# A decode step with sliding-window attention and an MLP on one Trainium2 core: fewer loads for the last weights, more loads for a bias, and a new order of the closing products

## The chip, the core and the metric

The kernel runs on one core of a Trainium2 chip (trn2). The metric is the device time of one execution in microseconds (us). Engines: PE multiplies matrices, PEld is its weight load, DVE, ACT and POOL work element by element, SP (SyncE) issues DMAs. A DMA is cut into packets that 16 DMA engines move.

## What is computed

Eight tokens (batch 8, one position, width 448) go through two branches, and a gate mixes them.

```python
g = sigmoid((x * gate_w).sum(-1, keepdims=True))
q = (x @ wq)                                  # 16 heads of 256
k, v = k_cache[:, :, -1024:], v_cache[:, :, -1024:]   # 8 KV heads, each for 2 query heads
a = (softmax(q k^T / 16) v) @ wo              # wo is 4096 x 448
b = gelu(layernorm(x) @ w1 + b1) @ w2 + b2    # hidden width 1792
out = g * a + (1 - g) * b
```

Weights and caches are bfloat16. The two windows of the caches are 67 MB of the 77.85 MB that the profile shows moved.

## The kernel before

**Loads.** All large loads go through SP's queue, in the order of a list called `plan`. A load fills a slot; a slot is 32 KB on each of 128 partitions (4 MB in all), and four slots form a ring (`RING = 4`, lines 98 to 118). `pump()` issues loads until four slots are ahead of what has been consumed; `done()` counts a slot as consumed and calls `pump()`. The plan is: wq (three DMAs), the eight blocks of keys k0 to k7, from k4 on with the values between them (k4, v0, k5, v1, k6, v2, k7, v3), then v4 to v6, w1 in two DMAs, v7 together with w2, and last wo. `rows_loader` (lines 138 to 146) issues one DMA for each piece of a list; line 143 is the issue.

**wo** is cut by `wo_v` (line 153) into four blocks q = 0 to 3, and each block into eight groups j = 0 to 7: on each partition a group is one row of 448 numbers (896 bytes), 112 KB over 128 partitions. The list `cuts` (lines 172 to 179) makes eight DMAs of it: block 0, block 1, groups 0 to 3 and 4 to 7 of block 2, and of block 3 the groups 0 to 1, 2 to 5, 6, and 7.

**Biases.** `biases()` (lines 193 to 201) is called after the keys k1 have been turned, just behind the issue of v0. It loads b2 into eight partitions with two DMAs of four rows each (line 195) and b1 with four DMAs of one row each (line 201). They are first used by `norm()` (line 318), called after the values of batch 4.

**DMA semaphores.** Every DMA names a semaphore that tells of its landing. The framework gives out eight of them; in the trace they are 100, 102, 103, 104, 105, 108, 109 and 110. The stretch around the biases and the last loads, from the trace's records of instructions and semaphore updates (us from the start of the span; "landed" is the last update before the next use):

| DMA | issued | semaphore | landed |
|---|---|---|---|
| k3 | 15.47 | 100 | 51.71 |
| k4 | 31.38 | 102 | 61.38 |
| v0 | 42.88 | 103 | 71.06 |
| b2, two DMAs | 43.55, 44.12 | 104, 105 | 70.72, 70.91 |
| b1, first three | 44.43, 44.72, 45.02 | 108, 109, 110 | 70.31, 70.49, 70.67 |
| b1, fourth | 51.73 | 100 | 70.86 |
| k5 | 61.46 | 102 | 80.73 |
| v1 | 71.15 | 103 | 90.54 |
| wo blocks 0, 1 | 158.70, 159.08 | 109, 110 | 177.80, 179.94 |
| wo block 2, two halves | 159.56, 160.03 | 100, 102 | 181.01, 182.11 |
| wo block 3, groups 0-1, 2-5 | 161.64, 162.21 | 103, 104 | 182.71, 183.81 |
| wo block 3, group 6, group 7 | 171.97, 175.69 | 105, 108 | 184.09, 184.37 |
| out by ACT, out by SP | 185.13, 185.12 | 109, 110 | 186.37, 186.55 |

**The closing products** (lines 688 to 740). `chunks` is a list of 46 products that are all summed into the output: 14 with w2, then 32 with wo, block by block and group by group. The last `TAIL` of them are `narrow`, the others `wide`. A wide product is one matmul over 448 columns into `A1`; four in a row go to four groups of output partitions (`g = i % QD`). DVE then adds the bias into `accs` (line 719). A narrow product is two matmuls over 224 columns, into `A2[0]` or `A2[1]` as the list `part` says, and each of the four combinations has its own group of output partitions. `pick` times `accs`, in float32, brings the wide sum into the narrow one; it stands at place `EARLY` of the narrow list. When the products for `A2[1]` are done, DVE copies them to `early` (line 737), beside the rest of those for `A2[0]`; `res` (line 738) adds the two, and SP and ACT each store a half. `FILL` says after how many wide products how many extra matmuls into an unused tile (`run_on`, tile `warm`) are run; they compute nothing that is used.

Of the kernel before, what the change touches and what calls it, by code (L numbers as in the profile page):

```python
# [17 lines left out]
def kernel(  # L18
# [18 lines left out]
    NB, Sq, D = A_x.shape  # L37
# [8 lines left out]
    QD = 4  # L46
# [11 lines left out]
    QN = 512  # L58
# [6 lines left out]
    J8 = Dh // BL  # L65
    NQW = Hq // QD
# [6 lines left out]
    CK = SLOT // Dh  # L73
    KQ = W // (KS * CK)
    HR = GROUP * UR
    TAIL = 12
    SHIFT = 96
    EARLY = 4
    TURNED = {5: 3, 6: 3, 7: 3}
    FAR = -3.0e38  # L80
    FILL = {0: 3, 14: 5, 22: 4, 30: 1, 34: 1}
    qscale = float(Dh) ** -0.5

    xf = A_x.rearrange("b s d -> (b s) d")
# [28 lines left out]
    def add(key, loader):  # L113
        index[key] = len(plan)
        plan.append(loader)

    def slot(*key):
        return slots[index[key]]
# [49 lines left out]
    for b in range(KQ, NB - 1):  # L168
        add(("v", b), pair_loader(A_v_cache, b))
    add(("w12",), rows_loader([w1_m, w1_t]))  # L170
    add(("v", NB - 1), last_values)
    cuts = [(q, 0, J8) for q in range(NQW - 2)] + [
        (NQW - 2, 0, 4),
        (NQW - 2, 4, 8),
        (NQW - 1, 0, 2),
        (NQW - 1, 2, 6),
        (NQW - 1, 6, 7),
        (NQW - 1, 7, 8),
    ]
# [7 lines left out]
    b2_b = consts.tile([NB, D], BF16)  # L187
# [3 lines left out]
    )  # L191

    def biases():
        for o in range(0, NB, QD):
            nc.sync.dma_start(
                b2_b[o : o + QD, :],
                B_b2.rearrange("(o d) -> o d", o=1).to_broadcast([QD, D]),
            )
        parts = B_b1.rearrange("(t d) -> t d", t=QD)
        for t in range(QD):  # L200
            nc.sync.dma_start(b1_r[BL * t : BL * t + 1, :], parts[t : t + 1, :])
# [26 lines left out]
    for u in range(NG):  # L228
        o = u * BL
# [429 lines left out]
    for m in range(NK):  # L659
        transpose_keys(m, steps(m - KQ) if m >= KQ else {})  # L660
        if m == 1:
            biases()
        if m < KQ:
            turn_blocks(m + 1)
        if m == 0:
            gate()
        scores(m)
        if m % KQ == KQ - 1:
            top(m // KQ)
        if m >= KQ:  # L670
            values(m - KQ)
# [23 lines left out]
    ] + [(oP[:, c % J8, c // J8, :], w[:, c * D : (c + 1) * D]) for c in range(NCH)]  # L695
    wide, narrow = chunks[:-TAIL], chunks[-TAIL:]

    def run_on(n, m=QN):
        for _ in range(n):
            nc.tensor.matmul(  # L700
                warm[:, 0:m],
                lhsT=ident[:],
                rhs=slot("v", NB - 1)[:, 0:m],
                start=True,
                stop=True,
            )

    run_on(FILL[0])
    for i, (lhsT, rhs) in enumerate(wide):
# [7 lines left out]
        )  # L717
        run_on(FILL.get(i + 1, 0))
    nc.vector.tensor_tensor(accs[:], A1[:], b2s[:], op=ALU.add)
    narrow.insert(EARLY, (pick[:], accs[:]))  # L720
    part = [1, 0, 1, 0, 0, 1, 1, 0, 0, 0, 0, 0, 0]
    early = consts.tile([2 * BL, DO], F32)
    res = consts.tile([2 * BL, DO], BF16)
    for i, (lhsT, rhs) in enumerate(narrow):
        k = part[i]
        for h in range(2):
            g = 2 * k + h
            nc.tensor.matmul(
                A2[k][BL * g : BL * g + NB, :],
                lhsT=lhsT,  # L730
                rhs=rhs[:, h * DO : (h + 1) * DO],
                start=(k not in part[:i]),
                stop=(k not in part[i + 1 :]),
            )
        if 1 not in part[i + 1 :] and k == 1:
            run_on(1, QN // 2)
            nc.vector.tensor_copy(early[:], A2[1][2 * BL : P, :])
    nc.vector.tensor_tensor(res[:], A2[0][0 : 2 * BL, :], early[:], op=ALU.add)
    for h, eng in enumerate((nc.sync, nc.scalar)):
# [31 lines left out]
```

## Time and profile before

| | |
|---|---|
| median of 3 runs | 189.46 us (189.45 to 189.76) |
| the profiled execution's own time | 189.29 us |
| its span in the profile | 187.4 us |
| bytes moved, mean rate | 77.85 MB, 415 GB/s |
| PE, DVE, POOL, ACT busy | 67%, 50%, 43%, 39% of the span |
| mean granted TensorE clock | 0.851 |
| last load landed, end of the span | 184.37 us, 187.39 us |

All profile times count from the start of the span. The execution is 1.9 us longer than its span and 0.17 us under the median. A name such as `slot<-in_A_wo_dram` reads as written<-read; L143 is a line of the kernel; SPq is SP's queue of instructions.

### The profile page before, as it was taken

Reading aid. Unit: us, or ns where it says so; the run is one execution under the profiler, and the core shown is the slowest. Engines: PE = TensorE matmul, PEld = TensorE weight load, DVE = VectorE, ACT = ScalarE, POOL = GpSimd, SP = SyncE. Lnnn points to the kernel's source line nnn. Section 1 sums busy time; section 2 is a strip of 40 time slices with the busy share of each in tenths; the row PEclk is TensorE's granted clock in tenths of the full one; section 3 lists DMA queues with packets and bytes.
Section 4 is the critical chain, followed back from the end, with each engine's and each line's share of the span. In section 5 each row is a group of like instructions: output and inputs, shape, how many; then the busy total and the mean of one; then the engine's idle time right before and its main releaser. Section 6 shows DMA issues by size and latency. Waiting matters only on the chain.

```text
span 187.4 us, 2775 instructions
## 1 busy us (share of the span) xinstructions
PE 125.4 (67%) x1102; PEld 73.0 (39%) x1103; DVE 94.0 (50%) x161; ACT 72.4 (39%) x87; POOL 80.8 (43%) x157
## 2 busy tenths in 40 slices
PE   0252498998988988489877985984670167543983
PEld 0010485675756746253752572563120022111321
DVE  6602247664654566770662281493044982347611
ACT  2003379692855929740680373184025010001000
POOL 8401591671927639103996899299900000000000
PEclk9999579999999999756997899999576576855798
DMA  6999999999998999999999999999999999999991
GB/s 223 444 455 448 448 434 413 388 442 448 444 448 381 418 439 435 430 416 455 451 416 402 434 458 441 392 441 427 430 430 423 434 430 428 432 430 418 421 406 65
DMA packets 5443, 77.85 MB, mean 415 GB/s; under 512 B 540, under 2 KB 1080, under 8 KB 1848
## 3 DMA queue, kind: packets, MB, share of 16 engines
q1 hardware_dynamic: 5384, 77.68, 97.2%
q8 instruction: 8, 0.13, 0.2%
q10 hardware_dynamic: 48, 0.02, 0.0%
q14 instruction: 3, 0.02, 0.0%
HBM read 77.69 MB, written 0.01 MB: 415 GB/s over the span
## 4 chain that ended last, share of the span: by engine, by line
DMA 46%; PE 25%; ACT 12%; DVE 7%; POOL 5%; issue 2%; SPq 1%; POOLq 0%; ACTq 0%; DVEq 0%
DMA slot<-in_A_k_cache_dram 22%; PE ktp L390 15%; DMA slot<-in_B_w_dram 12%; DMA slot<-in_A_wo_dram 12%; ACT kt L394 9%; PE S_ps L465 7%; POOL kt L369 5%; DVE kt L396 3%; PE PO L550 2%; DVE B L355 1%; ACT E L489 1%; ACT other L489 1%; SPq L143 1%; DVE EB L505 1%; DVE E L503 1%
## 5 line engine op out<-in xcount | busy, mean ns | idle before, releaser
L369 POOL COPY kt<-B 32x128 f32<-32x128 f32 (+1 forms) x128 | 72.4, 566 | 42.8 <-PE S_ps L465 24.9
L390 PE MATMUL ktp<-ident_f,slot 128*128 128x128 f32 x456 | 64.6, 292 | 14.0 <-DMA slot<-in_A_k_cache_dram 5.9
L394 ACT COPY kt<-ktp 128x1024 bf16<-128x1024 bf16 x57 | 56.3, 1015 | 45.8 <-PE ktp L390 45.7
L390 PEld LDWEIGHTS ktp<-ident_f,slot 128*128 128x128 f32 x456 | 52.4, 148 | 27.7 <-ACT kt L394 11.3
L396 DVE COPY kt<-ktp 128x1024 bf16<-128x1024 bf16 x57 | 39.0, 689 | 32.0 <-PE ktp L390 31.6
L465 PE MATMUL S_ps<-kt,qw 128*16 128x512 bf16 x256 | 21.1, 458 | 12.1 <-POOL kt L369 9.3
L550 PE MATMUL PO<-slot,ET 128*16 128x512 bf16 x256 | 22.2, 508 | 6.6 <-DMA slot<-in_A_v_cache_dram 3.0
L355 DVE STREAM_TRANSPOSE B<-slot 128x512 f32<-128x512 f32 (+1 forms) x8 | 8.8, 1105 | 14.2 <-DMA slot<-in_A_k_cache_dram 9.7
L465 PEld LDWEIGHTS <-qw 128*16 128x16 bf16 x256 | 6.6, 92 | 23.8 <-issue 13.3
L550 PEld LDWEIGHTS <-ET 128*16 128x16 bf16 x256 | 7.9, 112 | 19.3 <-issue 12.9
L525 PE MATMUL sm<-EZ,perm 128*128 128x128 bf16 x8 | 2.0, 248 | 13.4 <-DVE EZ L512 13.4
L407 PE MATMUL S_ps<-slot,xw 128*8 128x512 bf16 x24 | 2.9, 618 | 10.7 <-DVE xw L254 7.1
L478 DVE TENSOR_REDUCE nmx<-S_ps 128x1 f32<-128x2048 f32 x2 | 4.6, 2292 | 9.8 <-PE S_ps L465 9.8
L565 DVE STREAM_TRANSPOSE T<-PO 128x512 f32<-128x512 f32 x8 | 5.7, 707 | 7.6 <-PE PO L550 7.6
L627 ACT ACTIVATE zb<-za 128x448 f32<-128x448 f32 x1 | 0.6, 576 | 18.8 <-DVE za L626 18.8
L489 ACT ACTIVATE E<-S_ps,nmx 128x1024 f32<-128x1024 f32 x2 | 4.1, 2031 | 9.7 <-DVE nmx L478 9.7
L525 PEld LDWEIGHTS <-perm 128*128 128x128 bf16 x8 | 0.8, 100 | 16.6 <-DVE EZ L512 16.6
L445 POOL COPY qw<-qt 32x64 bf16<-32x64 bf16 x8 | 2.2, 277 | 11.3 <-DVE qt L432 11.0
L533 DVE TENSOR_TENSOR ET<-sm,mask 128x512 bf16<-128x512 f32 x8 | 5.5, 687 | 1.1 <-PE sm L525 1.0
L432 DVE STREAM_TRANSPOSE qt<-qs 128x512 bf16<-128x512 bf16 x2 | 1.3, 690 | 8.8 <-ACT qs L429 8.8
L407 PEld LDWEIGHTS <-xw 128*8 128x8 bf16 x24 | 0.7, 100 | 12.0 <-POOL b_r L237 7.1
L700 PE MATMUL warm<-slot,ident 128*128 128x512 bf16 (+1 forms) x14 | 4.3, 392 | 0.1
(91 smaller groups left out, 69.0 us busy)
## 6 DMA issues: line engine op xcount, KB each, us to landing
slot<-in_A_k_cache_dram SPq DMA_DIRECT2D x8, 4096.0 KB, 24.6
slot<-in_A_v_cache_dram SPq DMA_DIRECT2D x8, 4096.0 KB, 30.0
slot<-in_A_wq_dram SPq DMA_DIRECT2D x1, 2048.0 KB
slot<-in_A_wo_dram SPq DMA_DIRECT2D x2, 896.0 KB
slot<-in_B_w_dram SPq DMA_DIRECT2D x1, 1568.0 KB
slot<-in_B_w_dram SPq DMA_DIRECT2D x1, 1344.0 KB
slot<-in_A_wo_dram SPq DMA_DIRECT2D x3, 448.0 KB, 22.1
slot<-in_A_wq_dram SPq DMA_DIRECT2D x1, 1024.0 KB
```

The costliest lines, as they stand in the source:

```text
L355: nc.vector.transpose(B[:].rearrange("p c w x -> p (c w x)"), kn[:, 0 : n * P],)
L369: nc.gpsimd.tensor_copy(words[BL * w : BL * (w + 1), BL * g : BL * (g + 1), 0:n, 0], B[BL * g : BL * (g + 1), :, w].rearrange("p c x -> p ...
L390: nc.tensor.transpose(words[:, c, :, 0], kn[:, o : o + P], ident_f[:])
L394: nc.scalar.copy(dst, src)
L396: nc.vector.tensor_copy(dst, src)
L465: nc.tensor.matmul(S_ps[BL * t : BL * t + HR, k * QN : (k + 1) * QN], lhsT=qf[:, o : o + HR], rhs=KT[0][:, x : x + n, :, j], start=False, ...
L478: nc.vector.reduce_max(nmx[:], S_ps[:], axis=AXIS.X, negate=True)
L489: nc.scalar.activation((E[:, 0:W], other[:])[u].rearrange("p (c k s) -> p k s c", k=KQ, c=NCK), S_ps[:].rearrange("p (k u s c) -> p u k s ...
L533: nc.vector.tensor_tensor(ET[:].rearrange("p c u a r -> p (c u) a r"), sm[:] .rearrange("p k (o r) -> p k o r", o=1) .to_broadcast([P, NCK ...
L550: nc.tensor.matmul(PO[BL * t : BL * t + Hq], lhsT=ET[:, c].rearrange("p u a r -> p (u a r)"), rhs=vn[:, c], start=(c < QD), stop=(c >= NCK ...
L565: nc.vector.transpose(T[:, 0 : NG * n], PO[:].rearrange("p u (e j) -> p u j e", j=J8))
L700: nc.tensor.matmul(warm[:, 0:m], lhsT=ident[:], rhs=slot("v", NB - 1)[:, 0:m], start=True, stop=True,)
```

## The change

wo comes in six DMAs: blocks 0, 1 and 2 whole, and of block 3 the groups 0 to 5, 6, and 7. b2 comes in four DMAs of two rows in place of two of four rows. The narrow list now has the 16 products of blocks 2 and 3, with `pick` times `accs` ahead of them; the products of block 2 go to `A2[0]` and `A2[1]` by turns, group 0 of block 3 closes `A2[1]`, and groups 1 to 7 go to `A2[0]`. Four fillers stand after the last wide product (there was one after product 30 and one after product 34), and the short filler stands after block 2.

```diff
-    TAIL = 12
+    TAIL = 16
-    EARLY = 4
+    EARLY = 0
-    FILL = {0: 3, 14: 5, 22: 4, 30: 1, 34: 1}
+    FILL = {0: 3, 14: 5, 22: 4, 30: 4}
...
-    cuts = [(q, 0, J8) for q in range(NQW - 2)] + [
-        (NQW - 2, 0, 4),
-        (NQW - 2, 4, 8),
-        (NQW - 1, 0, 2),
-        (NQW - 1, 2, 6),
+    cuts = [(q, 0, J8) for q in range(NQW - 1)] + [
+        (NQW - 1, 0, 6),
         (NQW - 1, 6, 7),
         (NQW - 1, 7, 8),
     ]
...
     def biases():
-        for o in range(0, NB, QD):
+        for o in range(0, NB, 2):
             nc.sync.dma_start(
-                b2_b[o : o + QD, :],
-                B_b2.rearrange("(o d) -> o d", o=1).to_broadcast([QD, D]),
+                b2_b[o : o + 2, :],
+                B_b2.rearrange("(o d) -> o d", o=1).to_broadcast([2, D]),
             )
...
-    part = [1, 0, 1, 0, 0, 1, 1, 0, 0, 0, 0, 0, 0]
+    part = [1] + [0, 1] * 4 + [1] + [0] * 7
...
+        if i == J8:
+            run_on(1, QN // 2)
         if 1 not in part[i + 1 :] and k == 1:
-            run_on(1, QN // 2)
             nc.vector.tensor_copy(early[:], A2[1][2 * BL : P, :])
```

## The prediction

> **What bounds the kernel now.** I read the page first, then the chain of waits, then SP's own waits and its timeline, and last the trace's packets and semaphore updates for the moments at which loads land.
>
> ```profile
> span 187.4 us, 2775 instructions
> ...
> DMA  6999999999998999999999999999999999999991
> ...
> q1 hardware_dynamic: 5384, 77.68, 97.2%
> ```
>
> The DMA engines are busy from the second slice to the last but one, and SP's queue alone holds them for 97.2% of the span. No engine of the first list is over 67%. So the stream of loads is the bound, and a moment in which it stands still is not won back. The landings say the same: k5, v1 and the blocks after them land 9.66 to 9.81 us apart up to the last values (80.73, 90.54, 100.20, 109.89 ... 158.36).
>
> The chain in its window from 139 us ends so:
>
> ```profile
> 139.89 22.30 DMA slot<-in_B_w_dram
> 162.19 0.02 issue
> 162.21 21.60 DMA slot<-in_A_wo_dram
> 183.81 0.04 issue
> 183.85 0.84 PE S_ps L728 x12
> 184.69 0.02 issue
> 184.71 0.38 DVE res L738
> ```
>
> The end is the landing of wo plus about half a microsecond of products, an addition and the store. Two places can therefore move the time: the rate and the gaps of the stream, and the piece behind the last landing.
>
> How SP feeds the stream stands in its waits between 40 and 72 us (total, times, longest), and in its timeline there:
>
> ```profile
> SPq L126 <- DMA slot<-in_A_k_cache_dram: 9.4, 1, 9.4
> SPq L134 <- DMA slot<-in_A_v_cache_dram: 9.1, 1, 9.1
> SPq L201 <- DMA slot<-in_A_k_cache_dram: 6.4, 1, 6.4
> ```
>
> ```profile
> 42.88 0.62 SPq L134 DMA_DIRECT2D slot<-in_A_v_cache_dram  x1
> 43.55 0.83 SPq L195 DMA_DIRECT2D b_b<-in_B_b_dram  x2
> 44.43 7.53 SPq L201 DMA_DIRECT2D b_r<-in_B_b_dram  x4
> 61.46 0.55 SPq L126 DMA_DIRECT2D slot<-in_A_k_cache_dram  x1
> 71.15 0.62 SPq L134 DMA_DIRECT2D slot<-in_A_v_cache_dram  x1
> ```
>
> The four loads of b1 take 7.53 us to issue, because the fourth waits 6.4 us for a load of keys with which it shares no data. What it shares is the semaphore: its number 100 was k3's, which landed at 51.71, and the load starts at 51.73. Then k5 waits 9.4 us for k4 (semaphore 102, landed 61.38), and v1 waits 9.1 us for v0 (103, landed 71.06). The eight semaphores go round, and **a DMA waits until the DMA eight places ahead of it has landed**. SP issues in order, so what stands behind waits too. Now this costs nothing: when k5 is issued at 61.46, v0 still has 9.6 us to run.
>
> **The change part by part.**
>
> *wo in six DMAs.* Block 1 takes 179.94 − 177.80 = 2.14 us. The halves of block 2 take 1.07 and 1.10, so one load saves 0.03. Groups 0-1 and 2-5 of block 3 take 0.60 and 1.10; six groups at the rate of block 1 take 6/8 x 2.14 = 1.61, which saves 0.09. Together −0.12 us at the last landing. SP's two spared issues (0.33 us each) lie where it is idle (158 to 176 us).
>
> *The closing products.* Wide products now end with block 1's (180.57, end of L711's group), then `accs` (0.62) is ready at about 181.25. PE passes four fillers until 181.6 (four took 1.04), and `pick` times `accs` (0.54) ends near 182.15. Block 2 lands near 182.1: at most 0.1 us late for eight products that need four steps of 0.095 us (the spacing of the pairs of L728), in front of a landing that comes 1.6 us later. That interval covers the added fillers and the short one. Without it, three more fillers would cost 0.65. Behind the landing T of the six groups, group 0 runs beside group 1 in another group of output partitions (as the first four matmuls of L728 started within 0.01 us), so group 7 starts at T + 0.04 + 6 x 0.095 = T + 0.61. It lands at T + 0.56 and could start at T + 0.60. That is +0.01; if the two don't run beside each other, +0.1. `early` ends at T + 0.04 + 0.26 + 0.05 + 0.39 = T + 0.74, before `res` can start at T + 0.90 (184.71 − 183.81), so it stays hidden by 0.16.
>
> *b2 in four DMAs.* By themselves two more issues of 0.26 us, on an SP that then waits anyway. But they move all that follows two places on in the round. Behind v0 on 103 come b2 on 104, 105, 108, 109 and b1 on 110, 100, 102, 103. The second b1 waits for k3 (51.71), the third for k4 (61.38), **the fourth for v0 itself, 71.06**. Queued behind it on SP is k5, whose slot was free before 61.4, and nothing else is left for the DMA engines. The gap, step by step: the fourth b1 is issued 71.08 to 71.33 (0.25 each now); k5 starts at about 71.42. From issue to the first packet, the trace shows 0.8 (the store: 185.12 to 185.91) to 1.0 (the first load: 0.73 to 1.74), and the first packets of an idle engine took 0.15 to 0.35 us longer than later ones. So the engines work fully from 72.2 to 72.8; I take 72.5.
>
> Now twelve of the sixteen engines start on k5 at 69.05 to 69.86, the other four at 70.19 to 70.71. The gap is 2.6 to 3.4 us for the twelve and 1.8 to 2.3 for the four. Which of them sets the end? v0's landings show twelve engines 1.3 us or more ahead of the last one; at the last load (183 to 184 us) only five are still 1.0 ahead, and nine lie within 0.35 of the last. Between, single engines lose about 1.4 us each around five packets of the queue "q8 instruction" (87.5, 103.8, 120.8, 139.6, 168.9), and fall back to the latest. After the gap all start level, and the engines that lose 1.4 later come last. For those the shift is 72.5 − 69.35 = 3.15. If no such loss followed, it would be 72.5 − 70.71 = 1.8. I take 3.1, nearest to what the packets of this trace did.
>
> The Trainium skill, page "DMA: Bandwidth & Descriptors", section "Latency and other measured facts", gives 0.6 us to the first byte of a load issued from SP. By it the restart would be 0.2 to 0.4 us earlier and the sum about 0.3 lower; the 0.8 to 1.0 of the trace decides.
>
> *Sum:* −0.12 + 0.01 + 3.1 = +3.0 on the profiled execution's 189.29, so 192.3. That execution lies 0.17 under the median of 189.46; between the two bases I write **192.4**.
>
> **The rivals.**
>
> 1. *The gap costs less* (chance 0.15). SP stalls, but the engines' later losses don't repeat, or fall on engines with time to spare: 1.8 − 0.1 on 189.46 gives 191.1, with the earliest restart 190.8. For it speaks that the lateness never exceeds that of the latest engine in the trace of before; against it, that four or more engines did lose over 1.1 us after 71 us.
> 2. *The gap costs more* (0.04). PE's granted clock drops to 0.5 in part of the last slices (the PEclk row has 5s and 7s there); shifted against the products, half speed adds 6 x 0.095 = 0.6 behind the last landing: 193.0. The latest restart (72.8) with 3.4 gives 193.3, with both 193.6.
> 3. *The round is not what I read from it* (0.09). If the fourth b1 does not share v0's semaphore, SP is free before 61.46 and only −0.12 + 0.01 is left: 189.3, within what can be told. For it: only the trace, not the code, shows who assigns semaphores. Against: every DMA from k3 on follows the round.
> 4. *Faster* (0.04). It needs rival 3's free SP, and a price per load in the stream of more than 0.19 us, since two loads are spared and 0.38 is 0.2%. Where it would be: at the end, each load paying its time from issue to first packet, 0.8 to 1.0. Two fewer give −1.6 to −2.0, 187.5. Against it: the halves of block 2 land 1.10 us apart, for 1.07 at block 1's rate, so the border costs 0.03. The Trainium skill, same page, section "Anatomy of one DMA — SWDGE (gpsimd) path", has for loads from GpSimd a fit of 2.0 us for each DMA plus its bytes over 436 GB/s; by that rule two fewer would bring 4.0 us. The landings of the two halves speak against it here.
>
> **How the numbers follow.** The forecast has 0.68; its own range is 191.6 (restart 72.2 and a loss after it of 1.0) to 193.3. Slower by over 0.2% (0.38 us, about what a measurement of this kernel can tell from no change) is 0.68 + 0.15 + 0.04, and a stall by another place in the round adds 0.01: 0.88. Same 0.08, faster 0.04. The range 190.8 to 193.6 takes in the forecast and rivals 1 and 2, 0.87 in all; the no-stall cases lie outside.
>
> **What would show it.** In SP's timeline the loads of b1 stretch from 45 to 71 us, k5 is issued near 71.4, and SP's wait at L201 for v0 is new, about 9.4 us. In the DMA row one slice near 72 us falls from 9 to about 4 or 5. k5 lands near 83.5, not 80.7, and the last load near 187.4. Wrong from the root would be k5 issued before 62 us; wrong in size, a last landing under 186.5. The closing part is right if the last landing and the start of `res` stay 0.3 to 0.4 us apart, and blocks 2 and 3 up to group 5 land 2.14 and 1.6 us after what precedes them.

## The result and the profile after

The changed kernel takes 195.41 us (median of 5 runs, 195.04 to 195.43), the kernel before 189.45 beside it: a ratio of 1.0305, 95% interval 1.029 to 1.032. It is slower, as forecast, but by 6.0 us and not by 3.0, and outside the range given. The profiled execution took 195.04 us, its span is 193.0.

The page of the changed kernel, the lines that answer to those of before:

```profile
span 193.0 us, 2790 instructions
...
DMA  6999999999999939999999999999999999999980
...
q1 hardware_dynamic: 5096, 77.68, 94.5%
```

The row of the DMA engines has one new hole, the 3 in the fifteenth slice (67.5 to 72.4 us). The windows of one microsecond show it better (columns: stretch, its length, busy time of PE, PEld, DVE, ACT and POOL, granted clock, DMA share, GB/s):

```profile
69.00:70.00 1.00, 0.83 (x8) 0.59 (x6) 1.00 (x1) 0.87 (x1) 0.92 (x3) 1.00 0.23 92
70.00:71.00 1.00, 0.65 (x4) 0.42 (x4) 1.00 (x2) 1.00 (x3) 0.92 (x3) 1.00 0.11 41
71.00:72.00 1.00, 0.89 (x8) 0.89 (x9) 0.91 (x2) 1.00 (x2) 0.87 (x4) 1.00 0.00 1
```

From 71 to 72 us the stream moves 1 GB/s. In the kernel before these three windows have 492 to 510; the last of them:

```profile
71.00:72.00 1.00, 0.87 (x8) 0.87 (x9) 0.93 (x2) 1.00 (x2) 0.90 (x3) 1.00 1.14 492
```

(A packet counts where it starts, so the share of a microsecond can be off by a packet.)

SP's waits and its timeline there:

```profile
SPq L198 <- DMA slot<-in_A_k_cache_dram: 15.8, 2, 9.4
...
SPq L198 <- DMA slot<-in_A_v_cache_dram: 9.5, 1, 9.5
```

```profile
45.03 26.23 SPq L198 DMA_DIRECT2D b_r<-in_B_b_dram  x4
71.38 0.55 SPq L126 DMA_DIRECT2D slot<-in_A_k_cache_dram  x1
72.03 0.62 SPq L134 DMA_DIRECT2D slot<-in_A_v_cache_dram  x1
```

The four loads of b1 (L198 now) take 26.23 us to issue instead of 7.53, two waiting for keys and the fourth 9.5 us for v0; k5 goes out at 71.38, forecast 71.42. The record of that fourth load names semaphore 103 for its own landing and waits for 103 first, the one that v0 has. The mechanism is the one forecast. The end of the chain shows a second loss, which was not:

```profile
188.68 0.28 PE S_ps L725 x2
188.95 0.02 issue
188.98 0.40 DVE early L735
189.38 0.04 issue
189.42 0.85 PE S_ps L725 x14
190.28 0.02 issue
190.30 0.38 DVE res L736
```

PE does the two matmuls of group 0, and stands still until the copy into `early` is done; only then come the 14 matmuls of groups 1 to 7. The timeline names what they waited for:

```profile
189.42 0.84 PE L725 MATMUL S_ps<-slot,oP 128*8 128x224 bf16 x14 [0.48 <-DVE early L735]
```

The last load lands at 189.20, `res` starts 1.10 us later, where it was 0.34.

So the 5.6 us of span divide like this (landings from the trace's semaphore updates, before to after):

| part | before | after | difference |
|---|---|---|---|
| landing of k5 | 80.73 | 84.30 | +3.57 |
| landing of wo's block 1 | 179.94 | 184.88 | +4.94, so +1.37 after k5 |
| block 1 to the last landing | 4.43 | 4.32 | −0.11 |
| last landing to the start of `res` | 0.34 | 1.10 | +0.76 |
| start of `res` to the end of the span | 2.68 | 2.68 | 0 |

Outside the span the profiled execution has 2.06 us, 0.15 more than before.

### The profile page after: what moved, and what is told of

Same layout as the page of the kernel before. It is cut to its first block, busy times and chain, and to the rows that moved or that the text cites. A ratio compares the mean times of both kernels' runs of the same rounds, so it can differ in the third digit from the quotient of the medians.

```text
span 193.0 us, 2790 instructions
## 1 busy us (share of the span) xinstructions
PE 123.7 (64%) x1109; PEld 71.8 (37%) x1109; DVE 95.7 (50%) x161; ACT 72.2 (37%) x87; POOL 80.5 (42%) x157
## 4 chain that ended last, share of the span: by engine, by line
DMA 38%; PE 24%; DVE 15%; ACT 13%; POOL 5%; issue 2%; SPq 1%; POOLq 0%; ACTq 0%; DVEq 0%
DMA slot<-in_A_k_cache_dram 25%; PE ktp L387 13%; DMA slot<-in_A_wo_dram 13%; ACT kt L391 8%; PE S_ps L462 6%; POOL kt L366 5%; PE PO L547 4%; DVE kt L393 3%; ACT E L486 2%; ACT other L486 2%; DVE EB L502 1%; DVE B L352 1%; SPq L143 1%; DVE nmx L475 1%; DVE E L500 1%
## 5 line engine op out<-in xcount | busy, mean ns | idle before, releaser
L387 PE MATMUL ktp<-ident_f,slot 128*128 128x128 f32 x456 | 63.5, 288 | 16.4 <-DMA slot<-in_A_k_cache_dram 6.5
L387 PEld LDWEIGHTS ktp<-ident_f,slot 128*128 128x128 f32 x456 | 51.3, 146 | 30.2 <-ACT kt L391 12.1
L697 PE MATMUL warm<-slot,ident 128*128 128x512 bf16 (+1 forms) x17 | 5.0, 414 | 0.0
```

Of the source, the lines that this page charges most:

```text
L387: nc.tensor.transpose(words[:, c, :, 0], kn[:, o : o + P], ident_f[:])
L697: nc.tensor.matmul(warm[:, 0:m], lhsT=ident[:], rhs=slot("v", NB - 1)[:, 0:m], start=True, stop=True,)
```

## The experiments

The theory after the result: the semaphores' round stops SP (about 4.9 us), the copy into `early` holds PE (0.75 us), and the two add up. The rival: the six loads of wo, or the mere number and shape of the small loads, carry the loss.

**Each half by itself.** The changed kernel with b2 as before:

```diff
-        for o in range(0, NB, 2):
+        for o in range(0, NB, QD):      # again two DMAs of four rows
...
```

> The changed kernel with b2 in two DMAs again. Theory (the round of eight semaphores): the fourth load of b1 waits for k3 again and not for v0, k5 is issued near 61.5 us, the gap near 72 us is gone. Of the +5.6 us of span only the closing is left: last landing 184.2 to 184.3 (two loads spared, -0.12), and 1.1 us from it to the addition into res, as in the changed kernel, for 0.34 before. Sum 189.45 - 0.12 + 0.75 = 190.1. Rival (the six loads of wo or the new products carry the loss): 194 or more.

Measured: 190.66 us, ratio 1.0054 (1.0035 to 1.0072). k5 is issued at 61.89, the hole is gone, and `res` starts 1.07 us after the last landing. That landing is at 184.77, half a microsecond later than expected; the next two runs with the same loads of wo and b2 had it at 184.43 and 184.48, so this is no steady part of the cost. The rival is out.

The kernel before with b2 in four DMAs and nothing else (the same lines the other way round):

> The kernel before with b2 in four DMAs, nothing else. Theory: k5 is issued near 71.4, the DMA row has a gap from 69 to 74 us, the last load lands 4.95 later (the 4.83 of the changed kernel without the 0.12 that two spared loads bring), the closing stays at 0.34: 194.3 to 194.5. Rival (loss from the loads of wo): 189.5 to 189.9.

Measured: 195.02 us, ratio 1.0269 (1.0246 to 1.0292). k5 is issued at 71.89, the last load lands at 189.75, `res` starts 0.34 after it. The split of b2, which moves no byte more, is nearly the whole loss. It was 0.6 more than expected; k5 went out 0.51 us later than in the changed kernel (71.89 for 71.38).

**Place or number.** The kernel before with b2 in three DMAs:

```diff
-        for o in range(0, NB, QD):
+        for o, n in ((0, 3), (3, 3), (6, 2)):   # n rows each
...
```

> The kernel before with b2 in three DMAs (3, 3 and 2 rows). Theory: now k5 itself is the eighth DMA behind v0 and waits for its landing at 71.06; it is issued near 71.1, 0.3 earlier than with four, and the loss is almost the whole: 194.1. Rival (each DMA more costs its share, so that two more cost 4.9): about 191.9.

Measured: 194.11 us, ratio 1.0232 (1.0215 to 1.0249). Now SP waits for v0 at k5's own line, 9.4 us, and k5 goes out at 71.13:

```profile
SPq L126 <- DMA slot<-in_A_v_cache_dram: 9.4, 1, 9.4
```

By the ratios one DMA more costs 4.4 us and two cost 5.1 (4.55 and 5.46 by the medians): the price is not per DMA. With one instead of two it stays nothing:

> The kernel before with b2 in one DMA. Theory: k5 then stands in the round where it waits for k3 (51.7), v1 waits for k4 (61.4), and the two go out as soon as their slots are free; the queue is fuller, and nothing is gained, since the stream had no gap: 189.4 to 189.6, and no wait of SP for a load between 52 and 72 us but those for slots. Rival (the waits for k4 and v0 in the kernel before cost something): under 189.0.

Measured (`b2_b` loaded by one DMA of eight rows): 189.46 us, ratio 1.0003 (0.9994 to 1.0012). k5 goes out at 54.26, v1 at 65.75. The time is as expected; the waits are not. SP did still wait for k4 (6.6 us, v1) and v0 (4.8 us, k6), but with loads in the queue; an earlier issue bought nothing.

The changed kernel with all eight bias loads, b1's four behind k5:

```diff
...
         if m == 1:
             biases()            # b2's four
+        if m == 2:
+            biases_b1()         # b1's four
```

> The changed kernel with the same eight bias DMAs, but the four of b1 issued after the keys k2 have been turned, behind k5. Theory: k5 is then the fifth DMA behind v0 and goes out at 61.5 or before; the fourth b1 still waits for v0 at 71.06, but with k5 in the queue nothing stands still. Time as in the run with b2 in two DMAs, 190.1. Rival (the number or the shape of the small loads costs): 194 or more.

Measured: 190.18 us, ratio 1.0037 (1.002 to 1.0053). The fourth b1 still waits 9.5 us for v0, and it costs nothing, since k5 has gone out at 53.84:

```profile
SPq L200 <- DMA slot<-in_A_v_cache_dram: 9.5, 1, 9.5
```

The same wait in two kernels, 5 us in the one and nothing in the other: what counts is which load stands behind the waiting one, and whether the queue is empty by then.

**The closing.** The changed kernel, b2 in two DMAs, `A2[1]` in another tile:

```diff
...
-    A2 = [S_ps[:, k * QN : k * QN + DO] for k in range(2)]
+    A2 = [S_ps[:, 0:DO], PO[:].rearrange("p u d -> p (u d)")[:, 0:DO]]
```

> The changed kernel with b2 in two DMAs, and with A2[1] in the tile PO, which is free by then, instead of in S_ps beside A2[0]. Theory: the 14 last products wait for the copy into early only because the copy reads the tile that they write, though in another bank and other partitions; in another tile they start right behind group 0, and res starts 0.35 after the last landing, not 1.1. Against the changed kernel with b2 in two DMAs -0.75: 189.4 to 189.7. Rival (the products are held by PE itself or by their data): no change, 190.2 to 190.7.

Measured: 189.54 us, ratio 1.001 (1.0001 to 1.002). The chain's end in this kernel's timeline (line numbers two or three higher):

```profile
183.82 0.26 PE L728 MATMUL PO<-slot,oP 128*8 128x224 bf16 x2 [0.84 <-DMA slot<-in_A_wo_dram]
183.82 0.73 PEld L728 LDWEIGHTS <-oP 128*8 128x8 bf16 x15 [0.83 <-issue]
183.83 0.91 PE L728 MATMUL S_ps<-slot,oP 128*8 128x224 bf16 x14
184.12 0.39 DVE L738 COPY early<-PO 64x224 f32<-64x224 f32 x1 [2.81 <-PE PO L728]
184.77 0.38 DVE L739 TENSOR_TENSOR res<-S_ps,early 64x224 bf16<-64x224 f32 x1 [0.26 <-PE S_ps L728]
```

The 14 products start 0.01 us behind the two of group 0, the copy lies beside them, and `res` starts 0.34 after the last landing (184.43), not 1.10. (The median falls by 1.1 us from the 190.66 of the run with b2 in two, and by 0.6 from the 190.18 of the run with b1 later, which closes in the same way; the traces give 0.76.) The products had waited for a copy that read other columns and other partitions of their tile. The same kernel with `A2[1]` left in `S_ps` but closed by block 2:

```diff
...
-    part = [1] + [0, 1] * 4 + [1] + [0] * 7
+    part = [1] + [0, 1] * 4 + [0] * 8
```

> The changed kernel with b2 in two DMAs, and with group 0 of block 3 going to A2[0] too, so that A2[1] is closed by block 2 and copied before block 3 lands. Theory (PE waits for that copy): the copy lies under block 3's landing, PE starts at the landing of the six groups, and eight products of 0.095 us in a row end 0.1 later than in the kernel before: 189.5 to 189.8. Rival (PE waits for another thing): 190.2 to 190.7.

Measured: 189.74 us, ratio 1.0019 (1.0009 to 1.0028). The copy runs at 182.86, under block 3's landing, and `res` starts 0.36 after the last landing. Both ways take the second loss away, so it was that wait. What is left of the change then, six loads of wo for eight and the new order of the products, gains nothing: the two versions are 0.1 and 0.2% slower than the kernel before, with intervals just above 1.

**What the hole costs, and why more than forecast.** The kernel before with the eight bias loads one block of keys later, so that the hole comes ahead of v1, whose packets are 16 KB and not 32 KB:

```diff
...
-        if m == 1:
+        if m == 2:
             biases()            # b2 in four DMAs
```

> The kernel before with b2 in four DMAs and all eight bias loads one block of keys later, behind k5. Theory: the fourth load of b1 is now the eighth DMA behind k5 and waits for its landing near 80.7; v1 stands behind it, is issued near 81.0, and the gap moves to 79 to 84 us. The first packets of v1 are 16 KB, where those of k5 are 32 KB. If the slow restart (first packets 0.65 to 1.05 us longer than later ones) is a matter of the packet's size, about 0.4 is saved: 194.2. If it is a fixed time after an idle stretch: as with the gap before k5, 194.4 to 195.0. Rival (a wait in the round costs only at k5): 189.6.

Measured: 193.89 us, ratio 1.0238 (1.0225 to 1.0251), and the hole is where it was to come. That is 0.3 under the time forecast for a cost that goes with the packet's size, and 0.5 under the lowest for a fixed time. The four kernels with a hole, from the packets and landings of their traces (all times in us; "first packets": the first sixteen of the load behind the hole; "late": DMA engines that finish the last load within 0.8 us of the last one, the next being at least 1.1 us ahead):

| kernel | load issued | first packets start | they take | later ones take | last landing | q8 packets after the hole | late |
|---|---|---|---|---|---|---|---|
| changed kernel | 71.38 | 72.71 to 74.27 | 1.21 to 2.26 | 1.21 | 189.20 | 5 | 5 |
| b2 in four | 71.89 | 73.24 to 74.32 | 1.55 to 2.14 | 1.21 | 189.75 | 5 | 5 |
| b2 in three | 71.13 | 72.46 to 73.36 | 1.78 to 2.21 | 1.21 | 188.88 | 5 | 5 |
| hole ahead of v1 | 81.19 | 82.64 to 83.09 | 0.64 to 1.10 | 0.61 | 188.63 | 5 | 5 |

With packets of 32 KB the sixteen engines take 0.9 to 1.6 us to start one after another, and the first packet loses up to 1.05 us; with 16 KB it is 0.45 and up to 0.49. That agrees with the packet's size as a cause, though the place of the hole was changed with it; a run that changes the size alone was not made.

The last two columns are the other half. "q8 instruction" is a DMA queue of the page; its packets are 16 KB each, one engine at a time. What one costs can be read from the packets: in the traces of before, of the changed kernel and of the five runs that bear on this (b2 in four, b2 in three, the hole ahead of v1, the two with more PE below), a packet of q8 takes 0.88 to 0.97 us, and the packet of the load that starts as it ends takes 0.46 to 0.55 us longer than its neighbours. Together that is 1.42 to 1.44 us for all 60 of them, without the two that come in the last microsecond of a stream. To try whether these packets decide which engines are late, 70 idle matmuls of two columns were put ahead of each of the last four batches' values:

```diff
...
+        for _ in range(70):
+            nc.tensor.matmul(extra[:, 0:2], lhsT=ident[:], rhs=ident[:, 0:2], start=True, stop=True)
         values(b)
```

> The kernel before with b2 in four DMAs, as in the run with that edit alone, and with 70 idle matmuls of two columns (140 instructions of PE) ahead of each of the last four batches' values, 560 instructions in all. In the four runs with a gap, five packets of the queue q8 instruction come after it, and at the last load five of the sixteen DMA engines are late by 1 us or more against the rest. Theory (each such packet throws one engine back by about 1.4 us, and the late ones set the end): 2205 instructions of PE go with 8 packets, so 560 more bring 2: seven packets after the gap and seven late engines; the time stays within 0.5 of 194.9, since one late engine already sets the end. Rival (engines fall back for another reason): five late engines, whatever the packets.

Measured: 196.01 us, ratio 1.0348 (1.0331 to 1.0366), over the bound of 195.4. The profiled execution is the shortest of the four, 195.34. In it seven packets of q8 lie between the hole and the last landing (an eighth comes at 189.46, at the very end), and seven engines are late, by 0 to 0.67 us, the next being 1.46 ahead. The last landing is 189.67, where the run without the matmuls had 189.75. But `res` starts 0.79 after it, not 0.34: the added matmuls delay the closing products, the copy into `early` ends only at 189.62, and the last twelve matmuls wait for it as in the changed kernel. These 0.45 us belong to the profiled execution; the other three runs are 0.5 to 1.0 longer and have no trace, so the rest of the miss stays open.

> The kernel before with the same 560 idle instructions of PE and no other change. Theory: ten packets of q8, two engines more among the late ones at the last load (11 within 0.4 us of the last, where it was 9), time 189.3 to 189.7, since the engines thrown back were ahead by 1.4 us before. Rival (engines fall back for another reason): nine late engines; or, if the packets cost the stream as a whole, 0.1 us or more for each packet: 189.7 or more.

Measured: 190.97 us, ratio 1.0087 (1.0055 to 1.012): the expectation failed, in time and in the number of late engines. There are eleven packets of q8, where ten were expected. The load of v7 takes 10.89 us after the landing of w1 (162.41 to 173.30), 1.1 more than the 9.76 before, around a packet of q8 at 165.38; at the end one other engine is within 0.1 us of the last and all the rest are 1.1 or more ahead. I had assumed that the added packets hit engines with time to spare. One hit an engine that was among the latest, and the last landing moved by 1.35 us (185.72 for 184.37), with `res` 0.34 after it as before. With the 1.43 us that each packet takes from its engine, that speaks for the packets as the cause more strongly than what I had expected.

## Why the prediction was wrong, step by step

- **What bounds the kernel**: right. The hole in the stream was never won back.
- **b2 in four DMAs, the wait**: right to the tenth of a microsecond. The fourth b1 was issued at 71.04 (forecast 71.08), k5 at 71.38 (71.42).
- **The restart, the step that failed most.** "The engines work fully from 72.2 to 72.8; I take 72.5." From issue to the first packet it was 1.33 us, not 0.8 to 1.0, the engines started over 1.6 us and not together, and first packets took up to 1.05 longer, not 0.15 to 0.35. Taking from each first packet's end the usual 1.21, the engines work fully from 73.4 to 74.3, on average 73.8. The bounds were read from a load in packets of 4 KB and a store of 448 bytes each, and used for packets of 32 KB; they should have been widened upward. Some 0.2 us of the first term could have been read: SP's issuing instruction itself takes 0.55 us for k5, as the prediction's own lines show, but 0.32 for the store and 0.38 for the first load. From its end to the first packet it was 0.78 us for k5, against 0.50 and 0.63 (the store's first packet on SP's queue is at 185.94; 185.91 is ACT's half). Why this remainder is longer is not shown. The Trainium skill, page "DMA: Bandwidth & Descriptors", section "Latency and other measured facts", has 0.6 us to the first byte; counted from the start of the issue, as the prediction counts, that lies further off than the trace's rows.
- **Which engine sets the end**: right in kind. With the measured restart the prediction's own formula gives 73.8 − 69.35 = 4.45 for the average engine and 74.3 − 69.35 = 4.95 for the latest; block 1's landing moved by 4.94. That it meets the latest to a hundredth is luck: for b2 in four DMAs the formula gives 4.93 (average) and 5.53 (latest) where the last landing moved by 5.38, and for three 4.19 and 4.76 where it moved by 4.51. The five late engines, and seven with seven packets, bear out the losses after the hole, which rival 1 doubted.
- **wo in six DMAs**: −0.12 forecast, −0.11 measured, in part by chance. From block 1 to the last landing the changed kernel takes 4.32 us, the other four traces with six loads 4.38 or 4.39, and the traces with eight 4.37 to 4.43. By the fit of 2.0 us for each DMA plus its bytes, which the Trainium skill has on the same page, section "Anatomy of one DMA — SWDGE (gpsimd) path", for loads from GpSimd, two fewer would by estimate have brought 4 us. No load here is issued from GpSimd, so the fit itself is not tested; it does not carry over to SP's full queue.
- **The closing products**: +0.01 forecast, +0.76 measured. The step "`early` ends at T + 0.74, before `res` can start at T + 0.90, so it stays hidden by 0.16" asked only whether `res` would wait for the copy. PE did: group 1's products carry a wait on DVE's semaphore. The trace of before holds that wait already, in the same place and long fulfilled (the copy ended at 183.54, PE went on at 183.85 with wo's load), and the prediction did not ask who else waits for the copy. The copy itself ended where it was forecast, at T + 0.75 (189.38).
- **The range**: its upper end, 193.6, was made from the restart's too narrow bounds and a slower clock for the last products, which did not come (one of their matmuls took 0.26 us, as before). The sum on the way there is off too: with the latest restart (+0.3) and 3.4 for 3.1 (+0.3), 192.4 becomes 193.0, not 193.3; the 193.6 follows from 193.0 with the 0.6 of the slower clock. The two failed steps, the restart and the wait for the copy, are worth 1.8 and 0.75 us. That is the 2.6 between forecast and result in span (+3.0 and +5.6).

## What to carry to other kernels

Where a fixed set of semaphores goes round and one queue issues in order, count DMAs as places in the round: a few tiny loads more can make a large one wait for another's landing, harmless while something else is in flight when the wait ends, and dear when nothing is. Price the restart then by a load of the same packet size and by the engine that finishes last, not by the first byte. And where the order around a copy is changed, look up every instruction that waits for the copy, not only the one that reads it.

## What the runs showed of the hardware that was not expected

- A DMA stream that has run dry comes back slowly: with packets of 32 KB 1.33 to 1.35 us from issue to the first packet, 0.9 to 1.6 until all sixteen engines have one, and first packets of up to 2.26 us for 1.21.
- The sixteen engines of one queue don't stay level. Each packet of "q8 instruction" puts the engine that it falls on back by 1.43 us, and it does not catch up: in the run with more PE the engine that came last at 173.30 was still 1.1 us behind all but one at 185.72. Where the engine had time to spare this is hidden; where it was among the latest, the kernel pays, as one run shows. 560 more instructions of PE brought three such packets more and 1.5 us, in a kernel whose PE is busy 67% of the time.
